# Hashed attention and a gated MLP on one core: second halves of the first pair hashed in column tiles beside first halves of the second, and the first attention stage in a new order

## The chip, the cores and the metric

The kernel runs on one core of one Trainium2 chip. The metric is the device time of one execution in microseconds (us), lower is better. Beside it stands one execution with the hardware profiler on, whose rows give the start and length of every instruction on the engines: TensorE (PE, with its weight loads as PEld), VectorE (DVE), ScalarE (ACT), GpSimd (POOL) and SyncE (SP), which here only issues DMAs.

## What is computed

```python
q_bits = (einsum('bhsd,dk->bhsk', q, proj) > 0)          # 6 bits a token; k_bits likewise
mask = q_bucket[:, :, :, None] == k_bucket[:, :, None, :]
scores = where(mask, q @ k.T / sqrt(D), -1e9)
attn = softmax(scores) @ v                               # batch 4, heads 8, seq 768, head_dim 64
x = attn.transpose(0, 2, 1, 3).reshape(B * S, H * D)     # 3072 x 512
out = x + sigmoid(x @ w_res) * ((gelu(x @ w_gate) * (x @ w_val)) @ w_out)   # d_ff 1536
```

The hash of a token is the signs of six projections. Only keys in the same bucket as the query take part.

## The kernel before

**Pairs, halves and chunks.** Two heads of one batch are a pair; 16 pairs, four to a batch. The tokens of a pair, for q (side 0) and for k (side 1), lie as 12 tiles of 128 tokens; tiles 0 to 5 are the first head (the first half), 6 to 11 the second (the second half). A pair has nine score chunks of 1024 columns, and `PLAN` (L17) calls them S 0 to S 35 for the four pairs of batch 0. Each chunk is scored on PE (L500, two banks of 512 columns), goes through one exponential on ACT (L511), and its values product V (L475, eight small matmuls) is done later. The scores' PSUM tile `sp` has two buffers, so chunk n + 2 can be scored only when the exponential of chunk n has read its buffer. Closing a head takes one more matmul (`preset`, L447), and `finish` (L419, L420) normalizes it on DVE.

**From q and k to an operand of the scores.** `load` brings q or k of a pair from HBM (a queue on SP); the two heads of pair 0 come separately (`load_head`, L179). `tr` (L273, DVE) transposes 32x32 blocks of the fp32 input. A hash matmul multiplies that with the projection. The result is transposed back on DVE and compared with zero, which gives the bits as +-0.5, stored in columns 64 to 69 of a token-major tile `nat`, beside the input in bf16 (`cast`, L261 on ACT, L263 and L265 on POOL). `turn` then transposes the 71 columns on PE (L373) and `copy` brings the result from PSUM to the operand `aug` (L379 on ACT, L381 on DVE). Later pairs take a DMA transpose instead (`turn_dma`, L360). The bits make the mask: a mismatch lowers the exponent by so much that the exponential is nothing.

**Three ways to hash.** `hash1` (L318) hashes some tiles of one operand with a full-array matmul, and `bits1` (L323, L325) transposes back and compares. `hash` (`hash_mm`, L284) hashes whole operands of one or two pairs together: each operand (a "job") takes a column tile of 32 columns of the array, so two or four jobs run side by side; step 0 and 1 are the first half, 2 and 3 the second. `tokens` (L296) transposes back for all jobs at once and `bits` (L305) compares, one instruction for each 32 rows, on the engines named in the step. From batch 1 on, half of the operands get their bits by products on POOL (`product`, L335) and sums on DVE (`add_up`, L341) placed by the lists `PLACES`, `DRAIN` and `LAYS`.

**The order.** Nothing is scheduled automatically: each engine runs its instructions in the order in which the program issues them, and a waiting instruction holds all behind it on its engine, or on SP's queue. For batch 0 that order is `PLAN`, written out step by step; a step such as `('tr', 0, 1, 6, 12)` is a call of the function in `STEP` (L706). Letters behind a step name engines (v DVE, s ACT, p POOL, so 'vvp' goes round the three) or PSUM buffers ('av', 'r', 'f'). After `PLAN` comes the gate stage of batch 0, then for each further batch an attention stage of 36 slots with the residual and output matmuls of the batch before between the chunks, and a gate stage. `gate_val` (L529) does the gate and value products (L525, L542, L545), `project` (L551) the residual and output products (L557, L571) and the last sums (L574, L577). Before `PLAN`, the program fills PE with products of constants (`fill`, L229).

Of the kernel before, what the change touches and what calls it, by code (L numbers as in the profile page):

```python
# [9 lines left out]
FP32 = mybir.dt.float32  # L10
BF16 = mybir.dt.bfloat16
AF = mybir.ActivationFunctionType
ALU = mybir.AluOpType
# [16 lines left out]
    ('vs', 0), ('load', 4, 0), ('load', 5, 1), ('load', 4, 1), ('load_v', 3),  # L30
    ('S', 0),
    ('S', 1), ('hash1', 0, 1, 6, 12, 'av'), ('bits1', 0, 1, 6, 12), ('turn', 0, 0, 6, 12, 'av'),
    ('copy', 0, 0, 6, 12, 'v'),
    ('S', 2),
    ('S', 3), ('hash', (1,), 2), ('turn', 0, 1, 6, 12, 'f'), ('hash', (1,), 3), ('hash', (1,), 0),
# [758 lines left out]
```

## Time and profile before

| what | us |
|---|---|
| median of 3 runs (339.56 to 339.67) | 339.64 |
| the profiled execution | 339.34 |
| its span, from the first to the last instruction | 337.3 |
| PE busy in the span | 332.4 |
| DVE, ACT, POOL busy | 216.3, 213.8, 175.0 |

A row of a timeline has the start in us, the length, the engine, the line of the program, the operation, output and inputs by name, their shapes and the count of instructions merged in the row; in brackets how long the engine had been idle and what ended that. A row of a stretch of time has the busy time and count for each engine, the clock granted to PE, the busy share of the DMA engines and what they moved.

### The profile page before, as it was taken

What the parts mean: (1) busy time and instruction counts of PE and PEld (TensorE: products, weight loads), DVE (VectorE), ACT (ScalarE), POOL (GpSimd) and SP (SyncE); (2) the same over time, 40 slices, a digit from 0 to 9 for tenths busy, and PEclk for the clock granted to TensorE, in tenths of its full rate; (3) what the DMA queues carried; (4) which work ended last, traced back from release to release, by engine and by line L of the source; (5) the groups of instructions that cost most, each with busy time, mean ns of one, the idle gap of its engine ahead of it and who ended that gap; (6) DMA issues with size and microseconds to landing.
All of it is one profiled execution on the core that took longest, in us unless ns stands there. A gap on an engine that the chain in (4) does not pass through costs nothing.

```text
span 337.3 us, 7740 instructions
## 1 busy us (share of the span) xinstructions
PE 332.4 (99%) x3086; PEld 204.0 (60%) x3086; DVE 216.3 (64%) x458; ACT 213.8 (63%) x247; POOL 175.0 (52%) x260
## 2 busy tenths in 40 slices
PE   8999999999999999999999999999999999999996
PEld 7767665565666655565666665665566665666444
DVE  7977575554577958876577896876577444343243
ACT  4889962337999952437999982255999984322220
POOL 4779920235299943578799972567879100000000
PEclk9999999999999999999999999999999999999999
DMA  7998999999965223518068933825050340000012
GB/s 228 370 289 125 217 242 202 179 166 205 313 222 149 72 85 81 109 32 187 3 167 229 273 92 94 134 47 96 1 126 33 80 101 33 31 2 0 31 64 94
DMA packets 74387, 43.88 MB, mean 130 GB/s; under 512 B 52544, under 2 KB 71360, under 8 KB 74352
## 3 DMA queue, kind: packets, MB, share of 16 engines
q1 hardware_dynamic: 67872, 37.95, 45.3%
q0 software_dynamic: 6400, 5.44, 10.7%
q8 instruction: 24, 0.39, 0.5%
q14 instruction: 11, 0.09, 0.1%
q10 hardware_dynamic: 80, 0.00, 0.0%
HBM read 29.56 MB, written 6.29 MB: 106 GB/s over the span
## 4 chain that ended last, share of the span: by engine, by line
PE 83%; POOL 8%; ACT 4%; DVE 3%; issue 1%; DMA 1%; POOLq 0%; DVEq 0%; ACTq 0%
PE sp L525 37%; PE fps L571 14%; PE sp L500 14%; PE av L475 7%; PE rps L557 5%; POOL pr L335 4%; PE hs L284 3%; ACT ering L511 3%; ACT e L511 1%; PE wps L229 1%; PE pt L373 1%; POOL v L394 1%; DMA x_sb<-x_tok 1%; DVE sums L341 1%; POOL va L386 1%
## 5 line engine op out<-in xcount | busy, mean ns | idle before, releaser
L511 ACT ACTIVATE e<-sp 128x1024 bf16<-128x1024 f32 x117 | 117.7, 1027 | 8.6 <-PE sp L500 3.7
L335 POOL TENSOR_TENSOR pr<-ld,projr 128x384 f32<-128x384 f32 x96 | 93.8, 998 | 47.0 <-DVE sums L341 31.9
L542 ACT ACTIVATE gt<-sp 128x768 bf16<-128x768 f32 x48 | 38.9, 810 | 83.7 <-PE sp L525 80.0
L500 PE MATMUL sp<-aug,aug 71*128 71x256 bf16 (+1 forms) x384 | 86.0, 325 | 0.5
L571 PE MATMUL fps<-wo,hh 128*128 128x512 bf16 (+2 forms) x312 | 79.6, 362 | 0.0
L545 DVE TENSOR_TENSOR hh<-gt,sp 128x768 bf16<-128x768 bf16 x48 | 45.8, 954 | 42.9 <-PE sp L525 39.5
L525 PE MATMUL sp<-x_sb,wg 128*128 128x512 bf16 (+1 forms) x384 | 70.9, 326 | 0.0
L525 PE MATMUL sp<-x_sb,wv 128*128 128x512 bf16 (+1 forms) x384 | 70.9, 326 | 0.0
L475 PEld LDWEIGHTS <-e 128*128 128x128 bf16 x936 | 43.5, 97 | 25.9
L341 DVE TENSOR_REDUCE sums<-pr 128x6 f32<-128x384 f32 x96 | 50.2, 542 | 10.8 <-POOL pr L335 10.3
L525 PEld LDWEIGHTS <-wg 128*128 128x128 bf16 x384 | 37.1, 98 | 25.8 <-issue 1.5
L525 PEld LDWEIGHTS <-wv 128*128 128x128 bf16 x384 | 37.5, 98 | 24.9 <-issue 0.2
L475 PE MATMUL av<-va,e 128*128 128x65 bf16 x936 | 47.0, 193 | 0.0
L571 PEld LDWEIGHTS <-hh 128*128 128x128 bf16 x312 | 28.1, 97 | 21.6
L500 PEld LDWEIGHTS <-aug 71*128 71x128 bf16 x384 | 29.2, 97 | 11.6 <-issue 2.7
L574 DVE SCALAR_TENSOR_TENSOR fps<-th,fps 128x512 f32<-128x512 f32 (+2 forms) x26 | 17.0, 653 | 25.9 <-PE fps L571 25.8
L557 PE MATMUL rps<-wr,x_sb 128*128 128x512 bf16 x96 | 27.1, 379 | 0.0
L511 ACT ACTIVATE ering<-sp 128x1024 bf16<-128x1024 f32 x27 | 25.8, 1031 | 1.7 <-PE sp L500 1.4
L561 ACT ACTIVATE th<-rps 128x512 f32<-128x512 f32 x24 | 14.3, 594 | 18.7 <-PE rps L557 17.5
L273 DVE STREAM_TRANSPOSE t<-ld 128x768 f32<-128x768 f32 (+3 forms) x28 | 23.1, 843 | 1.7 <-DMA ld<-in_q_dram 1.0
L454 DVE COPY av<-av 128x390 f32<-128x390 f32 x24 | 13.6, 565 | 14.6 <-PE av L450 14.5
L263 POOL TENSOR_SCALAR nat<-ld 128x768 bf16<-128x768 f32 (+1 forms) x12 | 9.6, 804 | 19.3 <-DMA aug<-nat 17.4
(76 smaller groups left out, 257.4 us busy)
## 6 DMA issues: line engine op xcount, KB each, us to landing
ldv<-in_v_dram SPq DMA_DIRECT2D x16, 384.0 KB, 5.8
out_dram<-o SPq DMA_DIRECT2D x23, 256.0 KB, 2.3
ld<-in_q_dram SPq DMA_DIRECT2D x15, 384.0 KB, 5.6
ld<-in_k_dram SPq DMA_DIRECT2D x15, 384.0 KB, 5.8
wg<-in_moe_w_gate_dram POOLq DMA_DIRECT2D x4, 384.0 KB, 9.9
wv<-in_moe_w_val_dram POOLq DMA_DIRECT2D x4, 384.0 KB, 10.7
wo<-in_moe_w_out_dram POOLq DMA_DIRECT2D x3, 512.0 KB, 7.6
wr<-in_moe_w_res_dram POOLq DMA_DIRECT2D x1, 512.0 KB, 16.6
```

The source lines that it names most:

```text
L273: nc.vector.transpose(t32[p, side][:, sl].rearrange("p c h n -> p (c h n)"), raw[p, side][:, sl].rearrange("p c d -> p (c d)"))
L335: nc.gpsimd.tensor_mul(pr, raw[x][:, hi * T:(hi + 1) * T], projr[:, bit].unsqueeze(1).to_broadcast([P, T, D]))
L341: nc.vector.reduce_sum(sums[x][:, hi * T:(hi + 1) * T, bit], pr, axis=mybir.AxisListType.X)
L475: nc.tensor.matmul(av[p, hi][:, qt, :], e[:, off:off + P], va[:, hi, jt, 0:D + 1], start=first, stop=(repeats(p, hi) and jt == T - 1), ski ...
L500: nc.tensor.matmul(sp[:, off:off + nq * P], ks[0:KA, hi * T + jt, :], qs[0:KA, hi * T + qt0:hi * T + qt0 + nq, :], start=True, stop=True)
L511: nc.scalar.activation(e, sp, AF.Exp, scale=float(ALPHA))
L525: nc.tensor.matmul(sp[:, c0:c1], w[:, kk, bass.ts(m, P)], xs[:, kk, c0:c1], start=(kk == 0), stop=(kk == KM - 1))
L542: nc.scalar.activation(gt, sp[:, 0:S], AF.Gelu)
L545: nc.vector.tensor_mul(hidden[b][:, m, :], gt, ps[1][:, 0:S])
L557: nc.tensor.matmul(rps, x_sb[b][:, kk, t, :], wr[:, kk, :], start=(kk == 0), stop=(kk == KM - 1))
L571: nc.tensor.matmul(fps[:, cs], hh[:, m, bass.ts(t, P)], wo[:, m, cs], start=(m == 0), stop=(m == KF - 1))
L574: nc.vector.scalar_tensor_tensor(fps[:, cs], th[:, cs], 1.0, fps[:, cs], op0=ALU.add, op1=ALU.mult)
```

## The change

1. **Hashing.** `hash1` of the second halves of pair 0 (q and k) and `hash` of pair 1 go. In their place comes `hashp` (`hash_part`), in four steps. Steps 0 and 1 use four column tiles: second half of q and of k of pair 0, first half of q and of k of pair 1. Steps 2 and 3 use tiles 2 and 3 for the second halves of pair 1. `tokensp` transposes the two results back, and `bitsp` compares them: 32x36 elements an instruction for pair 0, 32x72 for pair 1.
2. **Order.** `PLAN` is written anew. Among its differences: POOL casts q of pair 0 (second half first, then first half) and k's first half before the copies of `proj` into `projw`; q of pair 1 is cast on ACT between S 0 and S 1; `hashp` 0 and 1 run between S 0 and S 1, `hashp` 2 and 3 after S 2; the first V moves from behind S 4 to behind S 3, and later ones stand further behind; the loads of k of pairs 2 and 3 come ahead of v of pair 1; the hash of pairs 2 and 3 is split over S 10 and S 12; q of pair 5 is cast on ACT behind S 35, ahead of the load of the Gelu table.
3. **Sums and bits.** `PLACES`, `DRAIN` and `LAYS` are new. Of batch 1's 48 products 16 instead of 21 stand in the gate stage, 13 instead of 8 in batch 2's attention stage, five of them in slot 0. Two `bits` steps beside the gate stage of batch 0 stand one column block earlier, and two loads in `LDY` move by one or two slots.

```diff
 PLAN = [
...
+    ('fill', 4, 70), ('tr', 0, 0, 4, 6), ('proj', 's', 'pssp'), ('fill', 44, 70), ('tr', 0, 0, 0, 4),
+    ('tr', 0, 1, 0, 2), ('cast', 0, 0, 'p', 6, 12), ('fill', 4, 70), ('tr', 0, 1, 2, 6),
+    ('cast', 0, 0, 'p', 0, 6), ('hash1', 0, 1, 0, 2, 'av'), ('bits1', 0, 1, 0, 2),
+    ('hash1', 0, 0, 4, 6, 'w0'), ('bits1', 0, 0, 4, 6), ('cast', 0, 1, 'p', 0, 6), ('tr', 0, 1, 6, 12),
+    ('load', 1, 0), ('hash1', 0, 0, 0, 4, 'av'), ('turn', 0, 1, 0, 2, 'f'), ('bits1', 0, 0, 0, 4),
+    ('copy', 0, 1, 0, 2, 's'), ('cast', 0, 1, 's', 6, 12), ('load', 1, 1), ('load_v', 0),
+    ('tr', 0, 0, 6, 12), ('proj', 'w', 'pppp'), ('turn', 0, 0, 4, 6, 'r'), ('cast', 1, 1, 'p'),
+    ('hash1', 0, 1, 2, 6, 'w1'), ('bits1', 0, 1, 2, 6), ('turn', 0, 0, 0, 4, 'r'), ('tr', 1, 0, 0, 6),
+    ('copy', 0, 0, 0, 4, 's'), ('tr', 1, 1, 0, 6), ('turn', 0, 1, 2, 6, 'f'), ('copy', 0, 0, 4, 6, 's'),
+    ('tr', 1, 1, 6, 12), ('copy', 0, 1, 2, 6, 's'), ('load', 2, 1),
+    ('S', 0), ('hashp', 0, 'av'), ('tr', 1, 0, 6, 12), ('cast', 1, 0, 's'), ('hashp', 1, 'av'), ('va', 0),
+    ('tokensp', 0),
+    ('S', 1), ('load', 3, 1), ('bitsp', 0, 0, 'vvp'), ('tr', 2, 1),
+    ('S', 2), ('hashp', 2, 'r'), ('hashp', 3, 'r'), ('turn', 0, 0, 6, 12, 'av'), ('bitsp', 0, 1, 'pv'),
+    ('tokensp', 1), ('load_v', 1),
+    ('S', 3), ('load', 2, 0), ('turn', 0, 1, 6, 12, 'f'), ('copy', 0, 0, 6, 12, 'v'),
+    ('copy', 0, 1, 6, 8, 'v'), ('bitsp', 1, 0, 'v'), ('V', 0),
+    ('S', 4), ('load', 3, 0), ('load_v', 3), ('copy', 0, 1, 8, 12, 'v'), ('V', 1), ('vs', 0),
+    ('bitsp', 1, 1, 'vp'),
...
+    ('S', 10), ('hash', (2, 3), 0), ('hash', (2, 3), 1), ('finish', 0, 0), ('load', 6, 0), ('va', 2),
+    ('hash', (2, 3), 2),
+    ('S', 11),
+    ('S', 12), ('copy', 1, 1, 6, 12, 'v'), ('tr', 5, 0), ('hash', (2, 3), 3), ('load', 4, 0),
+    ('tokens', (2, 3)), ('V', 5),
+    ('S', 13), ('V', 6), ('vs', 1), ('V', 7),
+    ('S', 14), ('cast', 3, 1, 'p'), ('bits', 2, 0, 'pv'), ('load', 6, 1), ('V', 8), ('bits', 2, 1, 'pv'),
...
+    ('S', 35), ('finish', 3, 0), ('V', 32), ('hash', (4, 5), 0), ('hash', (4, 5), 1), ('V', 33),
+    ('V', 34), ('cast', 5, 0, 's'), ('V', 35), ('open', 4, 0), ('cast', 4, 1, 'p'), ('preset', 4, 0),
+    ('gelu',), ('gv', 0), ('tr', 6, 0), ('va', 4), ('finish', 3, 1), ('tr', 7, 1), ('xturn', 3),
...
+    def hash_part(i, tag):
+        h, dh = divmod(i, 2)
+        key = "part", h
+        if key not in hsum:
+            hsum[key] = (av_ps if tag == "av" else mm_ps).tile([P, T, 32], FP32, tag=tag, name="hs")
+        units = [(0, 0, 1), (0, 1, 1), (1, 0, 0), (1, 1, 0)] if h == 0 else [None, None, (1, 0, 1), (1, 1, 1)]
+        for j, unit in enumerate(units):
+            if unit is not None:
+                p, side, hh = unit
+                nc.tensor.matmul(hsum[key][32 * j:32 * j + 32], projw[:, dh, :],
+                                 t32[p, side][:, hh * T:hh * T + T, dh, :], start=(dh == 0), stop=(dh == 1),
+                                 tile_position=(0, 32 * j))
+
+    def tokens_part(h):
...
+        n = 64 * h
+        nc.vector.transpose(htok["part"][n:, h].rearrange("p c n -> p (c n)"),
+                            hsum["part", h][n:].rearrange("p c n -> p (c n)"))
+
+    def bits_part(p, side, engs):
+        ht, j = htok["part"], 2 * p + side
+        for a in range(4):
+            rows = slice(32 * j, 32 * j + 32), slice(NBITS * a, NBITS * (a + 1))
+            dst = nat_of((p, side))[32 * a:32 * a + 32, :, D:D + NBITS]
+            if p == 0:
+                dst, src = dst[:, T:HT], ht[rows[0], 0, :, rows[1]]
+            else:
+                dst, src = dst.rearrange("p (h c) n -> p h c n", h=2), ht[rows[0], :, :, rows[1]]
+            engs[a % len(engs)].tensor_scalar(dst, src, 0.0, 0.5, op0=ALU.is_gt, op1=ALU.subtract)
```

More of the change, by code (lines that the diff above doesn't have):

```diff
@@ L17 @@
 PLAN = [
-    ('load', 1, 0), ('load', 1, 1), ('load_v', 0), ('load', 2, 0), ('load_v', 1), ('load', 2, 1),
-    ('load', 3, 0), ('proj', 's', 'pssp'), ('proj', 'w', 'pppp'), ('cast', 0, 1, 'p', 0, 6),
[10 rows of a table removed]
[L30 to L35, printed above, removed]
[9 rows of a table removed]
-    ('S', 12), ('hash', (2, 3), 2), ('hash', (2, 3), 3), ('copy', 1, 1, 6, 12, 'v'), ('cast', 2, 1, 'p'),
-    ('cast', 2, 0, 'p'), ('hash', (2, 3), 0), ('hash', (2, 3), 1), ('finish', 0, 0), ('tokens', (2, 3)),
-    ('bits', 2, 0, 'vvp'), ('bits', 2, 1, 'vp'),
[6 rows of a table removed]
-    ('S', 19), ('bits', 3, 0, 'vvvp'), ('turn_dma', 3, 0), ('vs', 2), ('turn', 2, 1, 6, 12, 'f'),
[12 rows of a table removed]
-    ('S', 29), ('hash', (4, 5), 2), ('finish', 2, 0),
[7 rows of a table removed]
-    ('preset', 4, 0), ('tokens', (4, 5)), ('repeat', 4, 0), ('gv', 1), ('cast', 4, 1, 'p'),
+    ('fill', 4, 70), ('tr', 0, 0, 4, 6), ('proj', 's', 'pssp'), ('fill', 44, 70), ('tr', 0, 0, 0, 4),
[4 rows of a table added]
+    ('copy', 0, 1, 0, 2, 's'), ('cast', 0, 1, 's', 6, 12), ('load', 1, 1), ('load_v', 0),
[5 rows of a table added]
+    ('tokensp', 0),
+    ('S', 1), ('load', 3, 1), ('bitsp', 0, 0, 'vvp'), ('tr', 2, 1),
+    ('S', 2), ('hashp', 2, 'r'), ('hashp', 3, 'r'), ('turn', 0, 0, 6, 12, 'av'), ('bitsp', 0, 1, 'pv'),
+    ('tokensp', 1), ('load_v', 1),
[9 rows of a table added]
+    ('S', 10), ('hash', (2, 3), 0), ('hash', (2, 3), 1), ('finish', 0, 0), ('load', 6, 0), ('va', 2),
+    ('hash', (2, 3), 2),
[22 rows of a table added]
+    ('S', 29), ('finish', 2, 1), ('hash', (4, 5), 2), ('load', 7, 0), ('vs', 4),
+    ('S', 30), ('V', 27), ('load_v', 6), ('V', 28),
+    ('S', 31), ('load', 7, 1), ('hash', (4, 5), 3),
[6 rows of a table added]
+    ('tokens', (4, 5)), ('repeat', 4, 0), ('gv', 1),
 ]
@@ L83 @@
     (1, 'tokens', (6, 7), True), (4, 'cast', 6, 0, 'p'), (5, 'cast', 6, 1, 'p'), (7, 'cast', 7, 0, 'p'),
-    (6, 'cast', 7, 1, 'p'), (7, 'bits', 6, 0, 'v'), (7, 'turn_dma', 6, 0), (10, 'bits', 6, 1, 'v'),
-    (10, 'turn_dma', 6, 1), (9, 'bits', 7, 0, 'v'), (9, 'turn_dma', 7, 0), (10, 'bits', 7, 1, 'v'),
+    (6, 'cast', 7, 1, 'p'), (7, 'bits', 6, 0, 'v'), (7, 'turn_dma', 6, 0), (9, 'bits', 6, 1, 'v'),
+    (10, 'turn_dma', 6, 1), (8, 'bits', 7, 0, 'v'), (9, 'turn_dma', 7, 0), (10, 'bits', 7, 1, 'v'),
     (10, 'turn_dma', 7, 1),
@@ L128 @@
-    DRAIN = {1: ('a', 2, 16), 2: ('a', 3, 20)}
-    LAYS = {1: [('g', 1, 7), ('g', 1, 8), ('a', 2, 5), ('a', 2, 17)], 2: [('g', 2, 7), ('g', 2, 8), ('a', 3, 6), ('a', 3, 21)]}
+    PLACES = {1: [('a', 1, 9), ('a', 1, 9), ('a', 1, 9), ('a', 1, 11), ('a', 1, 13), ('a', 1, 14), ('a', 1, 16), ('a', 1, 17), ('a', 1, 17), ('a', 1, 18), ('a', 1, 18), ('a', 1, 21), ('a', 1, 22), ('a', 1, 23), ('a', 1, 24), ('a', 1, 26), ('a', 1, 27), ('a', 1, 29), ('a', 1, 34), ('g', 1, 0), ('g', 1, 0), ('g', 1, 0), ('g', 1, 1), ('g', 1, 2), ('g', 1, 3), ('g', 1, 3), ('g', 1, 4), ('g', 1, 5), ('g', 1, 5), ('g', 1, 6), ('g', 1, 6), ('g', 1, 7), ('g', 1, 7), ('g', 1, 8), ('g', 1, 8), ('a', 2, 0), ('a', 2, 0), ('a', 2, 0), ('a', 2, 0), ('a', 2, 0), ('a', 2, 1), ('a', 2, 2), ('a', 2, 3), ('a', 2, 5), ('a', 2, 8), ('a', 2, 8), ('a', 2, 11), ('a', 2, 13)], 2: [('a', 2, 1), ('a', 2, 2), ('a', 2, 12), ('a', 2, 14), ('a', 2, 16), ('a', 2, 18), ('a', 2, 19), ('a', 2, 23), ('a', 2, 24), ('a', 2, 24), ('a', 2, 25), ('a', 2, 31), ('a', 2, 32), ('a', 2, 33), ('g', 2, 0), ('g', 2, 0), ('g', 2, 0), ('g', 2, 0), ('g', 2, 1), ('g', 2, 2), ('g', 2, 3), ('g', 2, 3), ('g', 2, 4), ('g', 2, 5), ('g', 2, 5), ('g', 2, 6), ('g', 2, 6), ('g', 2, 7), ('g', 2, 8), ('g', 2, 8), ('g', 2, 9), ('g', 2, 9), ('g', 2, 10), ('g', 2, 10), ('a', 3, 1), ('a', 3, 3), ('a', 3, 4), ('a', 3, 4), ('a', 3, 5), ('a', 3, 7), ('a', 3, 8), ('a', 3, 12), ('a', 3, 13), ('a', 3, 14), ('a', 3, 14), ('a', 3, 17), ('a', 3, 17), ('a', 3, 18)]}
@@ L130 @@
+    DRAIN = {1: ('a', 2, 17), 2: ('a', 3, 19)}
+    LAYS = {1: [('g', 1, 8), ('g', 1, 11), ('a', 2, 5), ('a', 2, 18)], 2: [('g', 2, 8), ('g', 2, 8), ('a', 3, 7), ('a', 3, 20)]}
     PRS = (1, 8)
@@ L286, in hash_mm @@
                                      tile_position=(0, 32 * j))
+    def hash_part(i, tag):
[11 more added lines that the diff above has]
+    def tokens_part(h):
+        if h == 0:
+            ht = hh_pool.tile([P, 3, HT // 3 + 1, 32], FP32, tag="ht", name="ht")
+            ht = ht.rearrange("p a c n -> p (a c n)")[:, 0:2 * (T + 1) * 32]
+            htok["part"] = ht.rearrange("p (h c n) -> p h c n", h=2, c=T + 1)[:, :, 0:T]
+        n = 64 * h
[11 more added lines that the diff above has]
+            engs[a % len(engs)].tensor_scalar(dst, src, 0.0, 0.5, op0=ALU.is_gt, op1=ALU.subtract)
     def hash_tok(jobs, psum=False):
@@ L721 @@
         w=load_w, load=load, load_v=load_v, xturn=lambda hp: x_turn(0, hp),
+        hashp=hash_part, tokensp=tokens_part, bitsp=lambda p, side, e: bits_part(p, side, [ENG[x] for x in e]),
         gelu=gelu_table, gv=first_gv)
```

3 lines of the change are left out of this document (1 added, 2 removed), and 69 rows, old and new, of the table PLAN.

## The prediction

> **What bounds the kernel now.** I read the engine totals of the page first, then the busy time by stretch of time, then each engine's timeline up to 50 us.
>
> ```profile
> PE 332.4 (99%) x3086; PEld 204.0 (60%) x3086; DVE 216.3 (64%) x458; ACT 213.8 (63%) x247; POOL 175.0 (52%) x260
> ```
>
> ```profile
> core 0: us, PE busy (x) PEld busy (x) DVE busy (x) ACT busy (x) POOL busy (x), PEclk, DMA share, GB/s
> ...
> 8.50:23.10 14.60, 14.59 (x206) 10.39 (x206) 12.10 (x27) 12.72 (x14) 10.92 (x20) 1.00 1.09 350
> 23.10:44.70 21.60, 21.23 (x328) 14.70 (x325) 14.60 (x36) 21.56 (x23) 20.13 (x35) 1.00 0.96 192
> ...
> 48.40:333.20 284.80, 284.55 (x2427) 169.26 (x2426) 178.16 (x362) 173.40 (x198) 139.77 (x187) 1.00 0.50 111
> ```
>
> PE is the bound nearly everywhere. From 48.4 to 333.2 us it is idle for 284.80 - 284.55 = 0.25 us (its ends are modelled, so small waits hide in this). The change gives PE the same work there, so behind 48.4 almost nothing can be won. The first attention stage is another matter: from 8.5 to 23.1 PE is full and ACT has gaps (12.72 of 14.60); from 23.1 to 44.7 ACT is full too (21.56 of 21.60). ACT's rows are the clock of that stage, because each of the 36 score chunks ends in one exponential (L511).
>
> ```profile
> 8.51 3.99 ACT L511 ACTIVATE ering<-sp 128x1024 bf16<-128x1024 f32 x4
> ...
> 13.68 4.84 ACT L511 ACTIVATE ering<-sp 128x1024 bf16<-128x1024 f32 x5 [0.91 <-PE sp L500]
> 18.41 1.94 ACT L511 ACTIVATE e<-sp 128x1024 bf16<-128x1024 f32 x2
> 20.63 1.94 ACT L511 ACTIVATE e<-sp 128x1024 bf16<-128x1024 f32 x2 [0.28 <-PE sp L500]
> 23.10 8.63 ACT L511 ACTIVATE ering<-sp 128x1024 bf16<-128x1024 f32 x9 [0.53 <-PE sp L500]
> ...
> 43.68 1.02 ACT L511 ACTIVATE e<-sp 128x1024 bf16<-128x1024 f32 x1
> 44.73 1.28 ACT L701 ACT_TABLE_LOAD   x1
> ```
>
> I call the exponentials e0 to e35. Two at 20.63 take 1.94 and one takes 1.02, so without a wait they start 1.94 - 1.02 = 0.92 apart. e0 starts at 8.51, e4 at 13.68, e13 at 23.10, e35 at 43.68. Without waits e4 to e13 would take 9 x 0.92 = 8.28; they take 9.42, so **1.14 us** are lost there. e13 to e35 would take 22 x 0.92 = 20.24; they take 20.58, so 0.34 are lost.
>
> **The change, part by part.** *PE work.* These are the rows of the hash, of a score chunk (S), of the value products (V, 16 for two chunks) and of transposes.
>
> ```profile
> 8.94 0.81 PE L318 MATMUL hs<-t,projs 128*128 128x192 f32 x4
> ...
> 11.93 1.17 PE L284 MATMUL hs<-t,projw 128*32 128x192 f32 x12
> 13.03 0.61 PE L500 MATMUL sp<-aug,aug 71*128 71x256 bf16 x3
> 13.48 0.65 PE L475 MATMUL av<-va,ering 128*128 128x65 bf16 x16
> 13.97 0.60 PE L500 MATMUL sp<-aug,aug 71*128 71x512 bf16 x3
> ...
> 20.96 1.51 PE L284 MATMUL hs<-t,projw 128*32 128x192 f32 x32
> ...
> 28.41 0.83 PE L373 MATMUL pt<-ident,nat 128*71 128x128 bf16 x12
> ```
>
> A row ends about 0.17 after the next may start. The 32 records of four column tiles are 8 steps in 1.51 - 0.17 = 1.34, that is 0.17 each; the 12 records of two tiles are 6 steps in 1.00, again 0.17; four records of the full array are 4 steps in 0.64. So a step costs the same whether one, two or four tiles ride on it. Before: 8 full-array steps for the second halves of pair 0 and 8 two-tile steps for pair 1, 16 in all. After: 4 four-tile and 4 two-tile steps. **8 steps, 8 x 0.165 = 1.3 us of PE, go.** Scores, values and transposes keep their counts; they only move.
>
> Whether those 1.3 us arrive depends on who is late, and in the new order that is first DVE, then ACT.
>
> *The start.* These rows say when the second heads of pair 0 land (the first answer covers the two issues above it) and when the eighth transfer lands, which is now k of pair 2.
>
> ```profile
> 1.74 0.43 SPq L179 DMA_DIRECT2D ld<-in_q_dram  x1
> ...
> 2.21 0.43 SPq L179 DMA_DIRECT2D ld<-in_k_dram  x1
> ...
> 4.18 0.47 SPq L161 DMA_DIRECT2D ld<-in_q_dram  x1
> ```
>
> ```profile
> DMA to landing us min/median/max: 3.3/3.8/4.2
> ```
>
> ```profile
> DMA to landing us min/median/max: 6.9/6.9/6.9
> ```
>
> q's second head lands at 1.74 + 3.3 = 5.0, k's at 2.21 + 4.2 = 6.4, the eighth transfer at 4.18 + 6.9 = 11.1. The DVE and POOL prices:
>
> ```profile
> 4.83 0.33 DVE L323 STREAM_TRANSPOSE hs<-hs 128x128 f32<-128x128 f32 x1 [0.17 <-PE hs L318]
> ...
> 5.29 0.25 DVE L323 STREAM_TRANSPOSE hs<-hs 128x64 f32<-128x64 f32 x1
> ...
> 5.67 0.57 DVE L273 STREAM_TRANSPOSE t<-ld 128x384 f32<-128x384 f32 x1
> 6.16 0.29 DVE L323 STREAM_TRANSPOSE wps<-wps 128x128 f32<-128x128 f32 x1
> ```
>
> ```profile
> 4.56 0.50 POOL L265 CAST nat<-ld 128x384 bf16<-128x384 f32 x1
> ```
>
> ```profile
> L305 DVE TENSOR_SCALAR nat<-ht 32x72 bf16<-32x72 f32 x17 | 3.7, 218 | 0.3
> ...
> L305 POOL TENSOR_SCALAR nat<-ht 32x72 bf16<-32x72 f32 x7 | 3.2, 456 | 2.3 <-DVE ht L296 1.8
> ...
> L323 DVE STREAM_TRANSPOSE hs<-hs 128x192 f32<-128x192 f32 x2 | 0.7, 370 | 0.0
> ...
> L261 ACT ACTIVATE nat<-ld 128x384 bf16<-128x384 f32 x2 | 1.0, 522 | 2.3 <-DMA ld<-in_k_dram 2.3
> ```
>
> A half transpose costs DVE 6.16 - 5.67 = 0.49, a `bits1` 5.29 - 4.83 = 0.46. `tokens_part` lies between 0.37 (the 128x192 row) and 0.57 (a half t transpose, twice as wide); I take 0.4, next to the row of its own width. `bits_part` for pair 0 writes 32x36, half of the 32x72 row: between 0.11 and 0.22 on DVE; I take 0.2, since so short an instruction is mostly fixed cost. Those on POOL (0.46 at most) end ahead of DVE's.
>
> POOL now casts q's second half first, so it waits until 5.0 and ends its three casts at 5.0 + 3 x 0.55 = 6.65; the first `turn` waits for the third. DVE has `tr(0,1,6,12)` ahead of `bits1(0,0,0,4)`, so it stands until 6.4, and from there runs without a gap: transpose 6.9, bits1 7.4, transpose 7.9, bits1 8.35, four half transposes of pair 1 10.3, tokens 10.7, three bits 11.3, `tr(2,1)` of k, landed at 11.1, 12.2, two bits 12.6, tokens 13.0, two copies (0.72) 13.7. Chunk 4 needs the last copy. In before S4 starts at 13.03 and e4 at 13.68, 0.65 later, so **e4 comes at 14.35 instead of 13.68, 0.67 late**. e0 to e3 lie earlier and hide: e0 at about 9.4, the cast of q of pair 1 now on ACT (0.8, at most 2 x 0.52), e1 at 11.0, e3 at 12.9. If the DVE cover went, ACT would have e4 at 13.8, so that cast alone is worth 0.1.
>
> *The rest of the stage.* In a slot of 0.92 PE spends 0.43 on S; 0.49 are left for other work, and the second score buffer lets S start some 0.15 early, so a slot with over 0.64 of other work delays the next exponential. V costs 0.25, a `turn` of six 0.34, a `hash` step pair 0.36. The new order has at most 0.65 in any slot from S5 on, but for S10, with three hashes: 1.1 - 0.64 = **0.45 lost**. Before had four in slot 12 and two V and a `turn` in slot 10. So e13 comes at 14.35 + 8.28 + 0.45 = 23.08, level with 23.10. Behind it no slot is overfull: I give back the 0.34 whole, e35 at 43.3. POOL's new order (`va(2)`, `vs(1)`, a cast, then the bits of pair 2) ends those bits about 24.8, 0.6 ahead of the `turn` that needs them, and cannot be moved much.
>
> *The tail.*
>
> ```profile
> 43.52 0.86 PE L284 MATMUL hs<-t,projw 128*32 128x192 f32 x16
> ...
> 45.05 0.33 PE L447 MATMUL av<-vsum,eps_sb 128*128 128x390 bf16 x1
> ...
> 48.45 1.51 PE L284 MATMUL hs<-t,projw 128*32 128x192 f32 x32
> ```
>
> From e35 to the hash that opens the gate stage it takes 48.45 - 43.68 = 4.77, and PE is full in most of it. V32 is now behind S35 too (0.25), but PE stands there for e35's end anyway. The cast of pair 5 on ACT (0.8) lies between e35 and the table load, so the table is in at e35 + 0.92 + 0.8 + 1.28 + 0.2 = e35 + 3.2, when PE is still in its second value product. I take 0.
>
> *Sums and bits.* 16 of batch 1's products instead of 21 lie in the gate stage, and five start slot 0 of batch 2. They are POOL and DVE work beside a full PE; five at 0.98 are 5 us, ahead of `vs` and `va` (2.9) that are needed 9 slots (10 us) later. Cost 0; without this cover at most 0.3.
>
> **Sum**: +0.67 (e4) - 1.14 + 0.45 (e4 to e13) - 0.34 (e13 to e35) = -0.36. The profiled execution takes 339.34 (span 337.3 and 2.0 around it), so 338.98; the median of the runs is 0.30 higher, 339.64, so **339.3**.
>
> **The rivals.** *PE's saving comes through* (338.5). `bits_part` at 0.11 takes 5 x 0.09 = 0.45 off DVE's chain, e4 comes at 13.9, and three hashes lose 0.25, because ACT left a score buffer ahead: 0.22 - 1.14 + 0.25 - 0.34 = -1.0, with 0.1 of waits less behind. For it: PE was full up to 23.1, and 1.3 of its work go. Against it: DVE is not shorter. *k of pair 2 is late* (340.6, slower). `tr(2,1)` stands in DVE's queue ahead of the bits and copies of pair 0 that chunk 4 needs. Each us that the transfer lands past 11.3 is a us of e4; past 11.7 the gain is gone, past 12.4 it is over 0.2% slower; one transfer later (1.1) and a second wait of that kind at S9 give +1.0. *The clock of PE.*
>
> ```profile
> 0.85 3.19 PE L229 MATMUL wps<-const-bfloat16-1.0 128*128 128x70 bf16 x52 [0.85 <-PEq L778]
> ```
>
> The warm-up products run at 3.19 / 52 = 0.061 for 70 columns, 0.88 ns a column; the transposes at 28.41 at 0.66 / 12 = 0.055 for 128, 0.43 ns. The half rate ends about 4.2, though the row of granted clock shows 9 throughout. The new order leaves PE idle from about 5.6 to 6.65 and again around 8. If that puts the full rate off by the length of the warm-up, hashes and first scores run at half rate, 1.5 us more ahead of e4: 340.8. [...] *The change does not show* (339.6): e4 is lost and only what S10 gives comes back.
>
> **How the numbers follow.** Forecast 339.3: 0.35. Does not show, 339.6: 0.07. Saving comes through, 338.5: 0.36. Late k, 340.6: 0.16. Clock, 340.8: 0.06. About 0.2%, 0.7 us, is what a measurement of this kernel can tell from no change. Faster by more: 0.36 and a little of the forecast's spread, 0.38; slower by more: 0.22; within: 0.40. The forecast's own range is 338.9 to 339.9. The whole range, 338.2 to 340.6, takes in both ends of the DVE prices (-0.45, +0.3 with tokens at 0.57) and the first case of late k.
>
> **What would show it.** e4 at 14.0 to 14.6 and DVE without a gap from 6.4 to 13.7 bear out the start; e4 at 13.7 or before refutes it. A gap of some 0.45 in front of e11, none over 0.15 behind e13, and the gate stage's first hash at 48.1 bear out the rest. Gaps of ACT behind e13, a PE gap over 0.3 past 48, or hash steps of 0.3 would make the prediction wrong.

## The result and the profile after

The changed kernel takes **352.86 us** (median; 351.02 to 359.3) against 339.65 before on the same chip: 1.0369 times the time, 95% interval 1.0342 to 1.0396. Runs over 1.5% slower than the fastest of their kernel (359.3 here, and below 349.28 in x1, 348.69 and 352.53 in x2, 361.92 in x4; mean granted clock 0.951 to 0.990) have no trace and are left out of the ratio and of the comparisons, so the ratio lies below the quotient of the medians. The forecast was 339.3. The profiled execution took 351.6 us with a span of 349.3.

The engine totals of the page after hardly differ in their shares, and hide what happened:

```profile
PE 337.2 (97%) x3086; PEld 205.4 (59%) x3086; DVE 218.5 (63%) x461; ACT 215.7 (62%) x248; POOL 175.5 (50%) x263
```

PE has the same number of records but 4.8 us more busy time, although 1.3 us of its work should have gone. Busy time that grows with less work says that the work ran slower. The busy time by stretch of time, after:

```profile
core 0: us, PE busy (x) PEld busy (x) DVE busy (x) ACT busy (x) POOL busy (x), PEclk, DMA share, GB/s
0.00:8.00 8.00, 5.68 (x72) 5.19 (x72) 4.92 (x21) 2.70 (x6) 3.69 (x18) 1.00 0.70 204
8.00:16.00 8.00, 6.72 (x74) 3.65 (x75) 7.58 (x22) 6.23 (x9) 5.58 (x12) 1.00 1.04 355
16.00:24.00 8.00, 6.65 (x92) 4.61 (x91) 7.83 (x14) 6.48 (x7) 6.89 (x13) 1.00 0.96 260
24.00:38.00 14.00, 14.00 (x230) 10.50 (x227) 10.95 (x26) 13.79 (x15) 11.36 (x22) 1.00 0.72 150
38.00:40.00 2.00, 0.17 (x6) 0.04 (x2) 0.78 (x3) 1.11 (x2) 1.92 (x5) 1.00 1.26 188
40.00:42.00 2.00, 0.00 (x0) 0.00 (x0) 0.00 (x0) 0.00 (x0) 2.00 (x5) 0.96 1.33 239
42.00:54.00 12.00, 11.91 (x100) 6.55 (x101) 1.64 (x3) 7.03 (x7) 4.23 (x6) 0.50 1.16 245
54.00:58.00 4.00, 4.00 (x67) 2.96 (x65) 2.18 (x5) 2.94 (x5) 0.00 (x0) 0.81 1.31 203
61.20:345.00 283.80, 283.74 (x2421) 169.14 (x2421) 177.85 (x362) 173.30 (x198) 139.87 (x187) 1.00 0.45 104
```

Three things stand here. DVE is nearly full from 8 to 24 us and PE is not (6.7 of 8). From 38.2 to 42.1 PE does nothing. Behind that, 100 records take 12 us at a granted clock of 0.50, where ahead of the wait 230 took 14 us. Behind 61 the kernel is as it was.

The exponentials on ACT (L511 before, L544 now) are the clock of the stage again. ACT's timeline, after:

```profile
31.68 2.85 ACT L544 ACTIVATE ering<-sp 128x1024 bf16<-128x1024 f32 x3
34.40 3.79 ACT L544 ACTIVATE e<-sp 128x1024 bf16<-128x1024 f32 x4
38.04 1.07 ACT L544 ACTIVATE ering<-sp 128x1024 bf16<-128x1024 f32 x1
43.20 1.02 ACT L544 ACTIVATE ering<-sp 128x1024 bf16<-128x1024 f32 x1 [4.09 <-PE sp L533]
44.93 1.02 ACT L544 ACTIVATE ering<-sp 128x1024 bf16<-128x1024 f32 x1 [0.71 <-PE sp L533]
46.55 1.02 ACT L544 ACTIVATE ering<-sp 128x1024 bf16<-128x1024 f32 x1 [0.60 <-PE sp L533]
```

The fourth row is e27, the first of pair 3: ACT stands 4.09 us for its scores. Each one behind it is some 1.7 us later than the one before, not 0.92. I add up both profiled executions from landmark to landmark. G is the first gate product, L558 (L525 before). The last column is a kernel of the experiments below, with two mends.

| stretch, us | before | after | both mends (z1) |
|---|---|---|---|
| start to e0 | 8.51 | 9.94 | 9.23 |
| e0 to e4 | 5.17 | 5.80 | 4.94 |
| e4 to e13 | 9.42 | 10.29 | 9.60 |
| e13 to e26 | 12.14 | 12.01 | 12.01 |
| e26 to e27 | 0.90 | 5.16 | 0.90 |
| e27 to G | 9.08 | 14.80 | 9.25 |
| G to the last instruction | 291.83 | 291.09 | 291.05 |

The differences of after are +1.43, +0.63, +0.87, -0.13, **+4.26, +5.72** and -0.74, together +12.04. Where the big ones come from is read on PE and SP. PE's timeline, after, at S 27:

```profile
37.76 0.41 PE L508 MATMUL av<-va,e 128*128 128x65 bf16 x8
42.09 1.01 PE L533 MATMUL sp<-aug,aug 71*128 71x512 bf16 x2 [3.92 <-DMA aug<-nat]
```

PE waits 3.92 us for a DMA: one of the two transposes of pair 3 (`turn_dma`, L360 before, L393 now). SP's queue, before and then after:

```profile
25.70 1.32 SPq L428 DMA_TRANSPOSE x_sb<-x_tok  x1
27.37 3.95 SPq L360 DMA_TRANSPOSE aug<-nat  x2
```

```profile
30.38 2.27 SPq L461 DMA_TRANSPOSE x_sb<-x_tok  x1
32.76 3.88 SPq L393 DMA_TRANSPOSE aug<-nat  x2
36.73 3.87 SPq L461 DMA_TRANSPOSE x_sb<-x_tok  x1
```

In both kernels the pair stands in SP's queue behind the transpose of the first finished heads (x_sb). It goes out 5.4 us later now: e13 is 2.9 us late, `finish` of these heads has moved from S 14 to S 17, and the bits of k that the pair needs from S 13 to S 18. Its second transpose also lands later after its issue. The answers to "how long from issue to landing" for these two instructions, before and then after:

```profile
DMA to landing us min/median/max: 3.8/4.1/4.4
```

```profile
DMA to landing us min/median/max: 3.7/5.7/7.7
```

After the change the second one, issued at 34.26, takes 7.7 us. A weight load of 384 KB, which stood at S 23 and now stands at S 16 of `PLAN`, goes out on POOL's queue near it. POOL's timeline, before and then after:

```profile
31.50 0.85 POOL L248 DMA_DIRECT2D wv<-in_moe_w_val_dram  x1
```

```profile
34.04 0.85 POOL L248 DMA_DIRECT2D wv<-in_moe_w_val_dram  x1
```

Before, the load was issued 1.5 us behind the second transpose (29.97), which landed in 3.8; after, it is issued 0.22 ahead of it.

The last loss is at the start. DVE's and then POOL's timeline, after, around `bits_part` (L319):

```profile
7.02 0.58 DVE L273 STREAM_TRANSPOSE t<-ld 128x384 f32<-128x384 f32 x1 [1.10 <-DMA ld<-in_k_dram]
...
11.48 0.57 DVE L319 TENSOR_SCALAR nat<-ht 32x36 bf16<-32x36 f32 x3
...
13.07 0.99 DVE L319 TENSOR_SCALAR nat<-ht 32x36 bf16<-32x36 f32 x2
...
15.29 0.87 DVE L319 TENSOR_SCALAR nat<-ht 32x72 bf16<-32x72 f32 x4
...
16.64 1.54 DVE L319 TENSOR_SCALAR nat<-ht 32x72 bf16<-32x72 f32 x2
```

```profile
12.85 0.99 POOL L427 TENSOR_TENSOR v<-ldv 128x384 f32<-128x384 f32 x1
...
16.42 0.83 POOL L263 TENSOR_SCALAR nat<-ld 128x768 bf16<-128x768 f32 x1 [0.35 <-PE sp L533]
17.20 0.99 POOL L248 DMA_DIRECT2D wg<-in_moe_w_gate_dram  x1
```

The first row is the landing of k's second head, for which DVE stands. Of the bits, three take 0.57 and four 0.87, about 0.2 each; but of the two at 13.07 the first takes 0.80, and the two at 16.64 take 0.66 and 0.87. Each of these three begins while a POOL instruction runs and ends where that ends (13.84, 17.25, 18.19).

### The profile page after: what moved, and what is told of

Read it like the earlier page. It is cut to its first block, busy times and chain, and to the rows that moved or that the text cites. A ratio compares the mean times of both kernels' runs of the same rounds, so it can differ in the third digit from the quotient of the medians.

```text
span 349.3 us, 7750 instructions
## 1 busy us (share of the span) xinstructions
PE 337.2 (97%) x3086; PEld 205.4 (59%) x3086; DVE 218.5 (63%) x461; ACT 215.7 (62%) x248; POOL 175.5 (50%) x263
## 4 chain that ended last, share of the span: by engine, by line
PE 85%; DMA 6%; POOL 5%; DVE 1%; issue 1%; SPq 1%; POOLq 0%; DVEq 0%
PE sp L558 36%; PE fps L604 17%; PE sp L533 15%; PE av L508 9%; PE rps L590 6%; DMA ldv<-in_v_dram 4%; DMA aug<-nat 2%; PE hs L284 2%; POOL v L427 1%; POOL pr L368 1%; POOL nat L338 1%; DVE sums L374 1%; SPq L179 0%; POOL va L419 0%; POOL v L429 0%
## 5 line engine op out<-in xcount | busy, mean ns | idle before, releaser
L544 ACT ACTIVATE e<-sp 128x1024 bf16<-128x1024 f32 x117 | 117.7, 1029 | 8.7 <-PE sp L533 3.6
L533 PE MATMUL sp<-aug,aug 71*128 71x256 bf16 (+1 forms) x384 | 89.5, 336 | 4.3 <-DMA aug<-nat 3.9
L558 PE MATMUL sp<-x_sb,wg 128*128 128x512 bf16 (+1 forms) x384 | 70.9, 326 | 0.0
L558 PE MATMUL sp<-x_sb,wv 128*128 128x512 bf16 (+1 forms) x384 | 70.9, 326 | 0.0
L558 PEld LDWEIGHTS <-wv 128*128 128x128 bf16 x384 | 37.5, 98 | 24.9 <-issue 0.2
L558 PEld LDWEIGHTS <-wg 128*128 128x128 bf16 x384 | 37.0, 98 | 25.6 <-issue 1.2
L533 PEld LDWEIGHTS <-aug 71*128 71x128 bf16 x384 | 29.6, 99 | 15.8 <-issue 6.5
L544 ACT ACTIVATE ering<-sp 128x1024 bf16<-128x1024 f32 x27 | 26.5, 1027 | 11.3 <-PE sp L533 11.3
L263 POOL TENSOR_SCALAR nat<-ld 128x768 bf16<-128x768 f32 (+1 forms) x11 | 8.5, 776 | 29.9 <-DMA aug<-nat 27.6
```

The costliest lines, as they stand in the source:

```text
L533: nc.tensor.matmul(sp[:, off:off + nq * P], ks[0:KA, hi * T + jt, :], qs[0:KA, hi * T + qt0:hi * T + qt0 + nq, :], start=True, stop=True)
L544: nc.scalar.activation(e, sp, AF.Exp, scale=float(ALPHA))
L558: nc.tensor.matmul(sp[:, c0:c1], w[:, kk, bass.ts(m, P)], xs[:, kk, c0:c1], start=(kk == 0), stop=(kk == KM - 1))
```

## The experiments

Theory: (1) the transposes of pair 3 land late, because they go out later and share the DMA engines with a weight load; (2) the idle PE loses its clock (granted 1.00 ahead of the wait, 0.50 behind it) and pays once more behind the wait; (3) DVE's bits are held by POOL, by the form of their source. Rivals: the wait is only that of a later issue; the slow PE behind it is bound by transfers and not by its clock; the bits are dear by their tile or place. Each kernel is compared with the kernel before on its own chip.

**x1, the weight load later.**

```diff
-    ('S', 16), ('w',), ('turn', 2, 1, 0, 6, 'f'), ...
+    ('S', 16), ('turn', 2, 1, 0, 6, 'f'), ...
-    ('S', 33), ('V', 30), ('V', 31), ('cast', 5, 1, 'p'), ...
+    ('S', 33), ('V', 30), ('V', 31), ('w',), ('cast', 5, 1, 'p'), ...
```

> Theory: chunk 27 waits 3.9 us because the DMA transpose of q of pair 3, issued at 34.26, shares the DMA engines with a weight load issued at 34.04 (it takes 7.7 us, the one before it 3.7), and that idle PE then loses half its rate until 55. With that weight load moved behind slot 33 the transpose lands some 4 us after its issue, near 38.3, the wait is under 0.5 us, no stretch runs at half rate, and the time falls by some 9.5 us to about 342. Rival, the transpose is late for its own issue on SP and not for the load: it still lands after 40, the wait is 2 us or more, the time stays over 347.

Measured: 341.85 and 342.42 (ratio 1.0078, 1.0045 to 1.0112). The transposes go out as late as in the changed kernel, and now land after 3.7 and 4.1 us; ACT has no wait from e26 on. Landing, SP's queue and ACT in this kernel:

```profile
DMA to landing us min/median/max: 3.7/3.9/4.1
```

```profile
30.23 2.06 SPq L461 DMA_TRANSPOSE x_sb<-x_tok  x1
32.40 3.35 SPq L393 DMA_TRANSPOSE aug<-nat  x2
```

```profile
34.26 3.79 ACT L544 ACTIVATE e<-sp 128x1024 bf16<-128x1024 f32 x4
37.90 8.54 ACT L544 ACTIVATE ering<-sp 128x1024 bf16<-128x1024 f32 x9
```

So the later issue alone cost nothing; the weight load just ahead of the second transpose did, and both big terms went with it. The traces of x3 and x4 below agree: there the load is issued 0.07 and 0.38 ahead, and the second transpose takes 7.5 and 9.0.

**x2, the transposes earlier.** They go ahead of the x_sb transpose, the weight load stays.

```diff
-    ('S', 17), ..., ('copy', 2, 1, 0, 6, 'v'), ('finish', 0, 1),
+    ('S', 17), ..., ('copy', 2, 1, 0, 6, 'v'), ('turn_dma', 3, 1), ('turn_dma', 3, 0), ('finish', 0, 1),
-    ('S', 19), ('turn_dma', 3, 1), ...
+    ('S', 19), ...
```

(`bits` of (3, 1) moves from S 18 to S 15, since the transpose needs it.)

> Both transposes of pair 3 are put ahead of the transpose of x in SP's order (the bits of k of pair 3 in slot 15 instead of 18), the weight load stays where it is. Theory of a late landing: both land before 36, chunk 27 does not wait, no half rate, about 342. Rival, the wait is the weight load's whatever the order: a wait of 2 us or more stays, with its half rate, over 347.

Measured: 341.64 and 340.93. Issued at 28.3 and 29.9, the transposes land 5.6 and 5.2 later, in time; e26 to e27 is 0.90. Either end of the collision can be moved. The load is issued at 34.06 here, 4.2 us behind them; why they take over 5 us all the same was not traced.

**x3, bits with an odd count.** The tile `ht` gets a padding so that the columns of the source are 3 by 2 and not one run of 6; pair 1 takes two instructions of 32x36 for one of 32x72.

```diff
-            ht = ht.rearrange("p a c n -> p (a c n)")[:, 0:2 * (T + 1) * 32]
-            htok["part"] = ht.rearrange("p (h c n) -> p h c n", h=2, c=T + 1)[:, :, 0:T]
+            ht = hh_pool.tile([P, 2, 3, 3, 32], FP32, tag="ht", name="ht")
+            htok["part"] = ht[:, :, :, 0:2]
```

> The bits of pairs 0 and 1 read a source whose outermost count is odd (3 groups of 2 tiles, with a gap), two instructions instead of one for pair 1. Theory of a lock between DVE and POOL: three bits on DVE (at 13.07, 16.64, 17.31, of 0.80, 0.66 and 0.87) end with the POOL instruction that runs beside them; with the odd source each takes about 0.2, e4 comes about 0.6 earlier and e13 about 2 earlier; the transposes of pair 3 and the weight load beside them move up together, so the wait of chunk 27 and the half rate stay, about 349.5. Rival, these bits wait for data of POOL: they stay at 0.7 and e13 stays at 26.

Measured: 350.28 and 350.07 (ratio 1.0316, 1.0286 to 1.0346); the wait of 4 us stays. e0 to e13 takes 14.46 instead of 16.09. DVE, then POOL, in this kernel:

```profile
13.31 0.38 DVE L315 TENSOR_SCALAR nat<-ht 32x36 bf16<-32x36 f32 x2
```

```profile
13.06 0.99 POOL L424 TENSOR_TENSOR v<-ldv 128x384 f32<-128x384 f32 x1
```

Two bits in 0.38 under the POOL instruction that held one for 0.80 before: the form of the source decides, not the tile or the place.

**x4, PE kept busy in the wait.** 17 products of constants, 512 columns each, ahead of S 27; they add work and change nothing that is computed.

```diff
+    ('keep', 17),
     ('S', 27), ('V', 24), ('V', 25),
```

> 17 products of constants of 512 columns (3.7 us) run on PE ahead of chunk 27, in the time in which it waits. Theory that the idle PE loses its rate: chunk 27 starts at about 42 as before, the granted clock stays 1.00, e27 to the first hash of the gate stage takes 12.3 instead of 18.0 us, about 346. Rival, the clock falls for another reason (the DMA load, the sparse start): the half rate stays and the time is 351 or more.

Measured: 347.25. e27 comes even later (44.05; the transpose took 9.0 here), but e27 to G takes 9.19 instead of 14.80, with the DMA share as high as in the changed kernel. By stretch of time, in this kernel:

```profile
38.00:42.00 4.00, 3.65 (x16) 1.48 (x15) 0.56 (x1) 0.88 (x1) 4.00 (x8) 1.00 1.56 194
42.00:46.00 4.00, 2.64 (x41) 1.70 (x41) 0.64 (x2) 1.95 (x3) 4.00 (x6) 1.00 0.96 205
46.00:54.00 8.00, 8.00 (x133) 5.47 (x127) 3.95 (x9) 7.98 (x9) 0.00 (x0) 1.00 1.21 263
```

The clock stays at 1.00, and 8 us hold 133 records where 12 held 100. The 5.7 us were the clock's, as far as this one execution shows.

**z4, the kernel before with an even count.** The opposite of x3, one edit in the kernel before, for theory (3):

```diff
-            ht = hh_pool.tile([P, 3, HT // 3 + 1, 32], FP32, tag="ht", name="ht")[:, :, 0:HT // 3]
+            ht = hh_pool.tile([P, 3, HT // 3, 32], FP32, tag="ht", name="ht")
```

> The kernel before with one edit: the token tile of the hash without its padding, so that the 18 columns of the source of a bits instruction make one dimension of even count, as in bits_part, and no longer 3 by 6. Nothing else changes. [...] Rival (the held bits of the changed kernel come from the place in its order or from 32x36 tiles): all rows stay at 0.17 to 0.25 and the time within 0.2% of before.

Measured: 339.83 against 339.50 (ratio 1.0018, 1.0004 to 1.0032). The seven bits of pair 1 on DVE, in the kernel before and then in this one, and POOL beside them in this one:

```profile
13.75 1.62 DVE L305 TENSOR_SCALAR nat<-ht 32x72 bf16<-32x72 f32 x7
```

```profile
14.05 2.33 DVE L305 TENSOR_SCALAR nat<-ht 32x72 bf16<-32x72 f32 x7
```

```profile
14.18 0.47 POOL L305 TENSOR_SCALAR nat<-ht 32x72 bf16<-32x72 f32 x1 [0.90 <-DVE ht L296]
14.73 1.03 POOL L394 TENSOR_TENSOR v<-ldv 128x384 f32<-128x384 f32 x1
15.84 0.49 POOL L396 TENSOR_TENSOR v<-v 128x128 f32<-128x128 f32 x1
```

One of the seven takes 0.88 and ends with POOL's instruction of 14.73, one takes 0.36 and ends with that of 15.84; the five others take 0.19 to 0.22, where each took 0.22 before. Theory (3) holds in the kernel before as well: the even form is a little quicker when it is free (0.19 to 0.22 against 0.22), and the two that end with a TENSOR_TENSOR of POOL take longer (0.88 and 0.36). Beside POOL's own bits (14.18, 0.47) none is held.

**y2 and a3, the sums alone.** The kernel before with the new `LDY`, `PLACES`, `DRAIN`, `LAYS` and the two bits steps, run twice, both times on chip 14 of the record.

> The kernel before with the new places of sums, lays, drains and of two bits of the gate stage alone; the order of the first attention stage is before's. In the changed kernel the stretches behind the gate's first hash are some 0.6 to 0.7 shorter than in before. Theory A (that is the sums' own gain): 338.8 to 339.1, with the first stage as in before (e35 at 43.7) and the gain behind 45. Rival B (it came from the late first stage, which left POOL and DVE ahead): no difference, 339.3 to 339.6.

> The kernel before with the new places of sums and bits alone, once more, beside the two others on one chip, to say which version is the fastest. If its gain is the sums' own: 338.5 to 339.1, ratio 0.996 to 0.999. If it was chance: 339.3 to 339.8.

Measured: 338.80 against 339.66 (ratio 0.9973, 0.9963 to 0.9982) and 339.05 against 339.80 (0.9982, 0.9973 to 0.9990). From G to the end it takes 291.13 and 291.12 instead of 291.83, as in every kernel that has these lists. **This version beats both kernels**, by 0.2 to 0.3% in both runs. The gain comes in six small places behind batch 0, of 0.06 to 0.32 each, less 0.20 lost at a seventh, at the same exponentials in all these kernels; which wait goes at each was not traced.

**y1 and y4, the hash alone.** In the order of before, `hashp`, `tokensp` and `bitsp` at the places of the old hash; y4 has the odd form and the new sums as well.

```diff
-    ('S', 1), ('hash1', 0, 1, 6, 12, 'av'), ('bits1', 0, 1, 6, 12), ('turn', 0, 0, 6, 12, 'av'),
+    ('S', 1), ('hashp', 0, 'av'), ('hashp', 1, 'av'), ('tokensp', 0), ('bitsp', 0, 0, 'v'), ('turn', 0, 0, 6, 12, 'av'),
+    ('bitsp', 0, 1, 'v'),
```

> The kernel before with the new hash alone: the four hash1 of the second halves of pair 0 and the four hash of pair 1 become hashp 0 to 3, with tokensp and bitsp as in the change, each at the place of the old ones; loads, casts, transposes, value work and sums stay in before's order. Eight PE steps of 0.165 go. Theory A (the loss of the change is not the hash's, it came from the order): the start gives some 0.3 to 1.0 of the 1.3, so 338.6 to 339.4, with no PE gap over 1 us and the clock at 1.0 throughout; one or two bits beside a POOL instruction are held to its end (0.6 to 0.9 instead of 0.2). Rival B (the new hash itself is dear, by its transposes and by bits that DVE and POOL can't run at once): slower than before by 0.5 to 2, 340.0 to 341.5, with e4 late as in the change (15.74).

> Before's order with the new hash (bits with an odd outermost count, so that POOL can't hold them) and the new places of the sums. If both parts gain by themselves and add up: 338.6 less 0.6, some 338.0 to 338.5, faster than both kernels. If the hash's step saving stays hidden behind ACT and DVE in before's order: the sums' gain alone, 338.8 to 339.1. If neither is worth anything in the old order: 339.3 to 339.7.

Measured: 345.62 (ratio 1.0170, 1.0131 to 1.0208) and 341.95 (1.0098, 1.0060 to 1.0136). My theory A of y1 fell, its rival holds, and more: against y2 on the same chip the new hash costs 3.15 us even without held bits. ACT's timeline in y4:

```profile
8.91 1.94 ACT L542 ACTIVATE ering<-sp 128x1024 bf16<-128x1024 f32 x2
13.84 1.94 ACT L542 ACTIVATE ering<-sp 128x1024 bf16<-128x1024 f32 x2 [2.99 <-PE sp L531]
```

One hash for both pairs waits for pair 1's transposes; pair 0's `turn` waits for that hash, its transpose back and four small bits on DVE, and S 2 is queued behind the `turn` on PE. In before e2 came at 10.56.

**y3 and z1, the changed kernel with two mends**: y3 is x2 with x3, z1 is x1 with x3.

> The changed kernel with both mends: the two DMA transposes of pair 3 ahead of the x_sb transpose on SP, and bits_part's source with an odd outermost count (3), two instructions of 32x36 for pair 1. Theory (wait, half clock and held bits are all that the change lost, and they add up): the kernel with the early transposes alone takes 341.3 by its two undisturbed runs, less 1.0 to 1.6 of held bits, so 339.7 to 340.3, within 0.2% of before, with e13 at 24.9 or earlier and no PE gap over 1 us. Rival (e13 to e26 is bound by something else, so that an earlier e13 is given back): 341.0 to 341.5.

> The changed kernel with bits_part's source odd in its outermost count and with the second weight load moved from S16 to S33 (the transposes of pair 3 stay behind the x_sb transpose). If the held bits and the wait with its half clock are separate and add up: the kernel with the late weight load alone had its gate stage at 48.05 and took 341.9 to 342.4; the odd bits took 0.9 to 1.1 off the gate's start in the two pairs of profiles that differ only by them, so gate at 47.0 and 340.8 to 341.5. Rival (the early transposes cost the kernel with both mends 0.6 at S18, by bits put ahead of a copy, and this one has none of that): gate at 46.4, 340.2 to 340.8.

Measured: 341.24 against 339.66 (1.0053, 1.0032 to 1.0074) and 340.37 against 339.50 (1.0037, 1.0009 to 1.0066). The time of y3 lies in the rival's range, and the rival is half right: e13 comes 1.38 earlier than in x2, the gate stage 0.94, because bits put ahead of a copy make S 18 wait 0.55 (e13 to e26 takes 12.70; 12.28 in x2, which has the same step, and 12.01 in z1, which has not). z1 is the changed kernel without the wait, the half clock and the held bits: of +12.3 us in the profiled execution nothing is left (339.31), of the median +0.9. Without the sums' gain of 0.75 to 0.86 in the medians, hash and order together would lose some 1.7.

**z2 and a1, the old hash in the new order**, in y3 and in z1.

```diff
-    ('S', 0), ('hashp', 0, 'av'), ('tr', 1, 0, 6, 12), ('cast', 1, 0, 's'), ('hashp', 1, 'av'), ...
+    ('S', 0), ('hash1', 0, 0, 6, 12, 'av'), ('tr', 1, 0, 6, 12), ('cast', 1, 0, 's'), ('bits1', 0, 0, 6, 12),
+    ('hash1', 0, 1, 6, 12, 'av'), ...
```

> The changed kernel with both mends (early transposes of pair 3), but the second halves of pair 0 hashed by hash1 and pair 1 by hash as before, at the places where hashp stood: 8 PE steps of 0.165 more, and on DVE two transposes with one 128x36 bits each (1.1) in place of one transpose and five 32x36 bits (1.3). Theory A (DVE's chain sets the start, PE has room): within 0.4 of the kernel with both mends, 340.8 to 341.6, e4 at 14.9 to 15.3. Rival B (PE's 1.3 were a real gain that other parts of the order ate): 342.0 to 342.6.

> The changed kernel with the late weight load and the old hash (hash1 for the second halves of pair 0, hash for pair 1, at the places where hashp stood), all else in the new order. The kernel with the late weight load, the new hash and odd bits took 340.37 with its gate stage at 45.93; the old hash in place of the new one took 1.0 off the gate's start where the transposes were early. Theory (the new hash is no gain in the new order either: DVE's five small bits and one transpose cost what PE's 8 steps save): gate at 44.9 to 45.6, 339.2 to 340.0. Rival (PE's 1.3 us are a gain once the waits are gone): gate at 46.5 to 47.2, 341.0 to 341.7.

Measured: 340.82 against 339.50 (1.0037, 1.0021 to 1.0054), and 341.06 against 339.80 (1.0059, 1.0037 to 1.0080). Against before on the own chip, the old hash gives +1.32 where the new one gave +1.58, and +1.26 where it gave +0.87. Theory A of z2 holds. a1 lies in its rival's range, but its profiled execution had e0 1.10 later than z1's, ahead of any part that differs; from e0 to the gate stage it takes 36.89 against 36.70. So in the new order the new hash, with its 1.3 us less on PE, gains between -0.3 and +0.4 us; the runs don't settle the sign.

**z3 and a2, pair 0 ahead of pair 1**, with the old hash: bits and copies of pair 0's second halves ahead of the transposes of pair 1 on DVE.

```diff
-    ('S', 3), ('load', 2, 0), ('turn', 0, 1, 6, 12, 'f'), ('copy', 0, 0, 6, 12, 'v'), ...
+    ('S', 2), ('turn', 0, 0, 6, 12, 'av'), ('turn', 0, 1, 6, 12, 'f'), ('copy', 0, 0, 6, 12, 'v'),
+    ('copy', 0, 1, 6, 8, 'v'), ('copy', 0, 1, 8, 12, 'v'), ('tr', 1, 0), ('tr', 1, 1), ('load_v', 1),
```

> As the last, but the old hash lets pair 0 go ahead: hash1 of both second halves behind S0, their bits and copies ahead of the transposes of pair 1 on DVE, which in the changed kernel had to come first because one hash takes both pairs. Theory A (the tie between the pairs costs the start: four half transposes of 0.5 and the landing of pair 1's loads stand ahead of pair 0's last bits): e4 at 13.0 to 13.9 instead of 15.07, and 339.5 to 340.5. Rival B (the loss lies in what else the order moved, casts and transposes ahead of e0): e4 gains no more than 0.3, 341 or more.

> As the last, with pair 0 let ahead of pair 1: on DVE the bits and copies of pair 0's second halves stand ahead of the four half transposes of pair 1, and the hash of pair 1 stands behind S4 and S5 on PE, so that S4 doesn't queue behind it (that was the fault of the earlier trial, where PE's queue held S4 for hash of pair 1). Theory (tying pair 0's last bits to pair 1's load and transposes is what the new hash costs at the start): e4 at 13.0 to 14.0 instead of 14.2 to 15.0. If nothing behind it is late, 338.4 to 339.4; if pair 1's bits, now late, hold S9, e9 comes at 19.5 or later and the time is 340 or more. Rival (the landing of q and k of pair 0 or ACT's cast sets e4): e4 at 14.2 or later.

Measured: 343.61 (1.0118, 1.0097 to 1.0139) and 347.86 (1.0253, 1.0222 to 1.0283); both hopes of a gain fell. z3 was ill made: the hash of pair 1 stood ahead of S 4 on PE (e4 at 17.27). In a2 e4 comes at 14.95, in the rival's range, because e0 is at 10.48; from e0 to e4 it takes 4.47 instead of 4.94 in z1 and 5.59 in a1, the full pace but for the cast on ACT. So untying the pairs helps pair 0, but pair 1 is late then: e11 comes at 29.25, 5.0 behind e10. PE stands 2.05 us there for a copy, and then its granted clock is 0.50 from 26.2 to 29.6. How the 1.7 us that are left divide between hash and order stays open.

## Why the prediction was wrong

**The failed step** is in "The rest of the stage": "Behind it no slot is overfull: I give back the 0.34 whole". It counted PE's work in each slot and did not follow SP's queue and the DMAs. That `turn_dma` of pair 3 goes out later, behind an x_sb transpose that moved from S 14 to S 17, and just behind a weight load that moved from S 23 to S 16, was priced at nothing; the list of differences under "The change" names none of these moves either. It cost 4.26 us of wait and 5.72 of half clock, 10 of 12. x1 and x2 show it from both sides, x4 parts the two terms.

**PE work.** 8 steps go, as said. But in before's order the new hash costs 3 us (y4 against y2), and in its own it is worth at most 0.4 (a1), since the start hangs on DVE and on what pair 0's bits wait for. The prediction had named that ("who is late, and in the new order that is first DVE") and yet forecast a gain.

**The start.** The order of DVE was right and so were its prices where nothing held it (bits 0.17 to 0.19 against 0.2, tokens 0.38 against 0.4). Two things were not: k's second head came at 7.02, not 6.4, and of five bits one took 0.80, to the end of a POOL instruction at 13.84. e4 came at 15.75, not 14.35. The bound "between 0.11 and 0.22 on DVE" was taken from bits of another source form; the form, not the size, was what mattered (the same 32x36 in x3: two in 0.38 beside POOL work).

**Slots up to e13.** S 10 was right: e10 to e11 takes 1.52, 0.60 lost against 0.45. A second place was missed: e6 to e7 takes 2.21, and still 1.45 in z1, where no bits are held. S 7 is queued there behind a `turn` of pair 1 that waits for a copy on DVE (PE stands 1.16 us for it, 0.28 in z1). With 9.60 from e4 to e13 instead of 8.73, the rule was 0.87 too kind even then.

**e13 to e35.** Dense up to e26 (12.01 for 13), as forecast; in z1 the whole stretch takes 20.44, so 0.14 of the 0.34 come back.

**The tail** was right within 0.2 (e35 to G takes 1.54 before, 1.72 in z1). **Sums and bits** were put at 0; they gain 0.7 in the profiled executions and 0.75 to 0.86 in the medians.

**The rivals.** k of pair 2 was not late: its transpose follows the bits on DVE without a wait (12.08). "The clock of PE" (its 0.06 was an estimate) was right that PE can run at half rate after standing still, but for this execution had the wrong place and size: it looked at gaps of 1 us at the start, and the half rate came behind the wait of 3.92 us at S 27. PE's timeline, after, three score chunks:

```profile
43.79 1.04 PE L533 MATMUL sp<-aug,aug 71*128 71x256 bf16 x3
...
54.03 1.04 PE L533 MATMUL sp<-aug,aug 71*128 71x256 bf16 x3
...
55.50 0.60 PE L533 MATMUL sp<-aug,aug 71*128 71x512 bf16 x3
```

A chunk takes 1.04 at 43.79 and at 54.03, and 0.60 at 55.50. By the clocks of the stretches above (0.96, 0.50, 0.81) PE was at half rate from 41.8 to 55.5, for 13.7 us, in which its rows were all but gapless (11.91 of 12 from 42 to 54). In a2 the half rate lasted 3.4 us, and it came after a wait of 2.05 us; in y1 a wait of 2.21 us took nothing back. So the half rate lasted 3.4 us in one execution and 13.7 in another, and of two waits of some 2 us only the shorter was followed by it; what decides was not found.

## What to carry to other kernels

When a step is moved, walk it through every queue that it uses, the DMA's too: a transpose that landed in 4 us took 8 when a weight load was issued just ahead of it, and it is the one operand that the next 9 chunks stand for. A PE wait of 4 us was paid twice here (4.26 and 5.72), and one of 2 us was followed by half clock in one of two cases, so price it with the half clock behind it, and fill it with dummy products if it can't be removed (x4: 9.19 instead of 14.80 from e27 to G). Look at the length of short DVE instructions beside POOL work: where one ends with POOL's instruction, try another form of its source. Here it was 3 groups of 2 columns for one run of 6, and two bits took 0.38 where one had taken 0.80.
